# A fused attention, MLP and routed-expert kernel on Trainium2: the first expert's fifth slice split 256+128, and eight products of a slice planned behind the rows' high part alone

## The chip, the core and the metric

The program runs on one NeuronCore of a Trainium2 chip. Its engines are TensorE (PE in the profile; PEld is its weight load), VectorE (DVE), ScalarE (ACT), GpSimd (POOL) and SyncE (SP, which here issues most DMAs). The metric is the time of one execution in microseconds, the median of several runs; lower is better.

## The reference, cut to what matters

Chunked attention feeds a dense MLP, and that feeds eight experts with a fixed capacity of 384 tokens each (3072 tokens, 512 features, 1024 hidden features per expert):

```python
x = attention(q, k, v, mem_k, mem_v)            # 3072 x 512
x = leaky_relu(x @ w_in) @ w_out                # hidden 2048
order = argsort(-(x @ w_gate).flatten())        # greedy: best (token, expert) first
for e in range(8):                              # an expert closes at 384 tokens
    out[mask[e]] = relu(x[mask[e]] @ w1[e]) @ w2[e]
```

## The kernel before

Every product in fp32 is made of three: each operand is split into a high and a low part (`winh`, `winl`, `x1h`, `x1l`, `gh`, `gl`), and high by high, low by high and high by low are added up in PSUM. The high part is an ACT copy, the low part a VectorE subtraction.

The program has two phases. The first (up to some 670 us) is attention and the dense MLP. The second, `phase2`, treats the eight experts one after the other and at the same time finds out which tokens each of them gets. For the next expert, `search(p)` narrows a threshold in six levels. A level is a round trip: VectorE compares (`d` L284 or L291, `cm` L301), TensorE counts (L318), VectorE decides (`lc` L325, `jk` and `am` L333, `fl` L336), TensorE spreads the result over the partitions (L340), and the next level's `d` reads that. After the last level come `which`, `above`, `full` and `fill` (L362 to L415), after which `prep` (L258 to L273, ending in `oh`) begins the next search as one uninterrupted piece of VectorE work. `tail(p)` turns the set `F` into ranks (L429), slots (L437 to L444), indices (L467 on TensorE, L475 to L479 on VectorE), gathers the rows (GpSimd), transposes them (L487) and splits them (L490 on ACT, L494 on VectorE).

An expert's hidden features come in eight slices `f` of 128. For a slice `load` fetches 512 KB of weights and splits them (L610 on ACT, L612 on VectorE), `gemm1` makes twelve products into a PSUM tile `ph` (L630) and evacuates it as `gh` (L637 on ACT) and `gl` (L639 on VectorE), and `gemm2` adds `gh` and `gl` times the second weights into the accumulators `po` (L655). There are two `ph` tiles; a `ph` comes free when the `gl` that read it is done. The expert's 384 tokens are three tiles of 128. For the first expert the third tile arrives later than the other two, so its first `FA` slices are computed in two passes, on 256 tokens and later on 128 (`egbh` and `egbl` are the evacuations of the short pass); the other slices run on 384.

The order on each engine is not written by hand. Every step is put down as an operation with an estimated duration, its dependencies and a key; `Plan.run` is a list scheduler that always starts, on the engine that is free first, the ready operation with the lowest key. Search and tail have keys around -1000, `load` about 200 + 8p + f - 6, `gemm1` 200 + 8p + f, `gemm2` two more. So weight splits of the second expert's first slices (202, 203) come before the evacuation of the first expert's fifth slice (204) when both are ready. The planner's estimates set the order alone; at run time each engine takes its instructions in that order and waits on semaphores.

Of the kernel before, what the change touches and what calls it, by code (L numbers as in the profile page):

```python
# [214 lines left out]
def phase2(tc, P, C, ident, L, x2d, we, out, ps_h, ps_o, ps_y, pools, lready, xready, open_pools, open_experts, room, roomy, X0, rows, r_xt, r_g):  # L215
# [9 lines left out]
    KD = DM // 128  # L225
# [5 lines left out]
    HOLD = 2.0  # L231
    LATE, SLACK = 0.5, 0.7
    SW = 0.08
    FA = 4
    V, G, S = nc.vector, nc.gpsimd, nc.scalar
    R = [dict() for _ in range(E)]
    A = {}
# [272 lines left out]
    X, XT = {}, {}  # L510
# [107 lines left out]
    def gemm1(p, f, lo=0, hi=TB):  # L618
        s = NF * p + f
        P.key = 200 + s  # L620
        w, o = W[p, f]
        xs = X[p]
        c, k = slice(lo, hi), hi - lo
        ph = ps_h.take()
        gh, gl = (r.take() for r in (r_gb if lo else r_g))

        def mm(n):
            a, x = ((0, 0), (1, 0), (0, 1))[n // KD]
            d = n % KD
            nc.tensor.matmul(ph.t[:, :k], w[a].t[:, d * 128:(d + 1) * 128], xs[x].t[:, d, c],  # L630
                             start=(n == 0), stop=(n == 3 * KD - 1))

        t = []
        for n in range(3 * KD):
            t = [P.op(("T", {128: 0.112, 256: 0.122, TB: 0.178}[k]), lambda n=n: mm(n),
                      [o[0], XT[p][lo // 128:hi // 128], t], [ph, *w, *xs])]
        a = P.op(("S", 0.42), lambda: S.activation(gh.t[:, :k], ph.t[:, :k], AF.Relu),  # L637
                 [t, [] if p else open_experts], [ph, gh])
        b = P.op(("V", 0.47), lambda: V.scalar_tensor_tensor(  # L639
            gl.t[:, :k], ph.t[:, :k], 0.0, gh.t[:, :k].bitcast(FT), op0=OP.max, op1=OP.subtract), [a], [ph, gh, gl])  # L640
        for i in range(lo // 128, hi // 128):
            GL[s, i] = gh, gl, 128 * i - lo, [a, b]
# [3 lines left out]
    def gemm2(p, f, tiles=range(TT)):  # L646
        s = NF * p + f
        P.key = 200 + s + 2
        w, o = W[p, f]
        if f == 0 and p not in ACC:  # L650
            ACC[p] = [r.take() for r in ps_o]

        def mm(i, n, gh, gl, at):
            l, a = ((gh, 0), (gh, 1), (gl, 0))[n]
            nc.tensor.matmul(ACC[p][i].t, l.t[:, at:at + 128], w[a].t[:, 512:1024],  # L655
                             start=(f == 0 and n == 0), stop=(f == NF - 1 and n == 2))

        for i in tiles:
            gh, gl, at, done = GL.pop((s, i))
            if p == E - 1 and f >= NF - 2:  # L660
                P.key = 200 + NF * p + NF + 1 + i + (f - NF) / 4
            for n in range(3):
                q = PREV[i] = P.op(("T", 0.235), lambda i=i, n=n, gh=gh, gl=gl, at=at: mm(i, n, gh, gl, at), [done[:1 + n // 2], o[1], PREV.get(i)],
                                   [ACC[p][i], gh, gl, *w])
            if f < NF - 1:
                continue
            y = ps_y.take()
            o2 = P.op(("S", 0.53), lambda i=i, y=y: S.activation(y.t, ACC[p][i].t, AF.Copy), [q], [ACC[p][i], y])

            def fn(i=i, y=y):  # L670
                if stores:
                    G.memset(rt([1, 1], FT, "spacer"), 0.0)
                st = G.indirect_dma_start(
                    out=out, out_offset=bass.IndirectOffsetOnAxis(ap=R[p]["idx"][:, i:i + 1], axis=0),
                    in_=y.t, in_offset=None)
                for other in stores:
                    tc.declare_no_dep(st.ins, other.ins, reason="a token has one expert: rows of other tokens")
                stores.append(st)

            o2 = P.op(("G", 1.04), fn, [o2], [y])  # L680
            P.dep(P.op(("D", 1.05), None, (), [y]), [o2], lat=1.6)


    for p in range(E):
        if p < E - 1:
            search(p)
        else:
            P.key = -1000 + 10 * p
            filled[p] = P.op(("V", 1.0), lambda: last(p), chain, after=[gathered.get(p - 2)])
        number(p)  # L690
        tail(p)
        first = []
        if p == 0:
            for lo, hi in ((0, TB - 128), (TB - 128, TB)):
                tiles = range(lo // 128, hi // 128)
                for f in range(FA + 2):
                    if f < FA:
                        if lo == 0:
                            load(p, f)
                        gemm1(p, f, lo, hi)  # L700
                    if f >= 2:
                        gemm2(p, f - 2, tiles)
            first = range(FA)
        for f in range(NF):
            if f not in first:
                load(p, f)
                gemm1(p, f)
            s = NF * p + f - 2
            if s >= 0 and s not in first:
                gemm2(*divmod(s, NF))  # L710
        if p == E - 1:
            gemm2(p, NF - 2)
            gemm2(p, NF - 1)
# [3 lines left out]
def kernel(ctx, tc, q, k, v, w, w_gate_t, we, out):  # L717
# [515 lines left out]
    def expert_pools():  # L1233
# [7 lines left out]
    rows.view = lambda x: x.rearrange("p a b -> p (a b)").bitcast(FT)  # L1241
    o2 = P.op(("X", 0.0), expert_pools, [[d if t < NTILE - 1 else d.queue for t, d in X2D], list(PREV.values())])
    phase2(tc, P, C, ident, L, x2d, we, out, r_h, r_o, r_x2, pools, ls, X2D, o1, o2,
           [x.rearrange("p a b -> p (a b)") for x in win],
           [[GT[s] for s in range(SL * NF, NJ * NF)] + [[], list(PREV.values())][f >= 3] for f in range(NF // 2)], [r.take() for r in r_x1], rows, r_x1, r_g)
# [57 lines left out]
```

## Time and profile before

| | us |
|---|---|
| median of 3 runs | 988.23 |
| lowest and highest run | 986.81 to 990.12 |
| the profiled execution, whole | 989.57 |
| its span from first to last instruction | 987.6 |
| TensorE busy in the span | 969.7 |
| VectorE busy | 771.1 |
| ScalarE busy | 444.0 |

The profiled execution took 1.97 us more than its span, and 1.34 us more than the median. The profile's page gives busy times, the span in 40 slices, the chain of work that ended last and the costliest groups; the trace gives the instructions of any stretch in order of time, what each waited for, and busy times with the granted TensorE clock for any stretch.

### The profile page before, as it was taken

The numbers are of one execution on the slowest core, as the hardware profiler recorded it, in microseconds if no ns is written. First come the engines' busy times: TensorE is split into PE (matmuls) and PEld (weight loads), VectorE is DVE, ScalarE is ACT, GpSimd is POOL, SyncE is SP. The second block draws the span as 40 slices with busy tenths as digits, with TensorE's granted clock in tenths as the row PEclk, the third lists the DMA queues.
The fourth block names the chain that finished last, engine by engine and source line by source line (L and its number), as shares of the span: only waits on it lengthen the run. The fifth ranks groups of instructions, "written<-read, shape, count | busy, mean of one in ns | idle before, by whom it ended". The sixth has DMA issues, their size and how long they took to land.

```text
span 987.6 us, 17321 instructions
## 1 busy us (share of the span) xinstructions
PE 969.7 (98%) x6070; PEld 839.8 (85%) x6070; DVE 771.1 (78%) x2577; ACT 444.0 (45%) x1191; POOL 128.3 (13%) x145
## 2 busy tenths in 40 slices
PE   9999999999999999999999999998999999999997
PEld 7778888888888888888888999777888888888996
DVE  7999798698698689689779984587899998877610
ACT  7777634444444544444554433023424433435511
POOL 0678521000000000000000000010120120220211
PEclk9999999999999999999999999998999999999999
DMA  8656520011111121121120000045452642635500
GB/s 270 219 203 234 187 60 30 30 64 58 30 62 42 47 63 30 56 66 31 49 73 12 1 1 1 33 139 171 129 174 74 223 161 75 235 113 174 184 33 33
DMA packets 36327, 95.50 MB, mean 97 GB/s; under 512 B 4368, under 2 KB 8464, under 8 KB 36112
## 3 DMA queue, kind: packets, MB, share of 16 engines
q1 hardware_dynamic: 32256, 81.54, 25.3%
q0 software_dynamic: 3840, 12.59, 3.8%
q8 instruction: 48, 0.79, 0.3%
q14 instruction: 39, 0.32, 0.1%
q10 hardware_dynamic: 144, 0.26, 0.1%
HBM read 81.79 MB, written 12.58 MB: 96 GB/s over the span
## 4 chain that ended last, share of the span: by engine, by line
PE 83%; DVE 8%; issue 4%; ACT 2%; POOL 1%; DMA 1%; POOLq 0%; DVEq 0%; ACTq 0%; SPq 0%
PE po L1064 24%; PE ph L970 23%; PE ph L630 13%; PE po L655 12%; PE pa L852 3%; DVE junk L1094 2%; PE pa L922 2%; PE pa L895 2%; DVE wp L947 1%; DVE wa L949 1%; DMA wst<-in_w_dram 1%; PE pt L487 1%; DVE wp L946 1%; ACT X L861 1%; PE pc L318 1%
## 5 line engine op out<-in xcount | busy, mean ns | idle before, releaser
L1094 DVE CUSTOM_DVE_ANT_0 junk<-x,wgb 128x512 bf16<-128x512 f32 x296 | 207.6, 701 | 5.4 <-DMA wgb<-in_w_gate_t_dram 1.0
L978 ACT ACTIVATE gs<-ph 128x384 f32<-128x384 f32 x128 | 62.7, 490 | 185.2 <-PE ph L970 181.5
L1064 PE MATMUL po<-wouth,gh 128*128 128x512 f32 x321 | 130.8, 408 | 1.1 <-ACT wouth L953 0.9
L1064 PE MATMUL po<-woutl,gh 128*128 128x512 f32 x321 | 127.7, 398 | 1.7 <-POOL woutl L954 1.7
L979 DVE TENSOR_TENSOR gs<-ph,gs 128x384 f32<-128x384 f32 x128 | 71.1, 556 | 72.4 <-ACT gs L978 71.6
L1064 PE MATMUL po<-wouth,gl 128*128 128x512 f32 x321 | 126.5, 395 | 0.7 <-POOL gl L981 0.6
L861 ACT ACTIVATE X<-X,st 96x128 f32<-96x128 f32 x248 | 96.7, 392 | 47.8 <-DVE st L856 47.6
L970 PE MATMUL ph<-x1h,winh 128*128 128x384 f32 x512 | 111.3, 339 | 0.0
L970 PE MATMUL ph<-x1h,winl 128*128 128x384 f32 x512 | 110.7, 337 | 0.2 <-POOL winl L954 0.2
L970 PE MATMUL ph<-x1l,winh 128*128 128x384 f32 x512 | 109.6, 335 | 0.0
L970 PEld LDWEIGHTS ph<-x1h,winh 128*128 128x128 f32 x512 | 91.7, 188 | 9.2
L637 ACT ACTIVATE gh<-ph 128x384 fp32r<-128x384 f32 (+1 forms) x64 | 31.0, 485 | 142.7 <-PE ph L630 131.1
L970 PEld LDWEIGHTS ph<-x1h,winl 128*128 128x128 f32 x512 | 92.0, 188 | 1.9 <-POOL winl L954 0.8
L970 PEld LDWEIGHTS ph<-x1l,winh 128*128 128x128 f32 x512 | 90.6, 188 | 0.5
L1064 PEld LDWEIGHTS po<-wouth,gh 128*128 128x128 f32 x321 | 60.3, 188 | 14.9 <-ACT wouth L953 1.6
L1064 PEld LDWEIGHTS po<-wouth,gl 128*128 128x128 f32 x321 | 60.2, 188 | 14.9 <-POOL gl L981 2.0
L1064 PEld LDWEIGHTS po<-woutl,gh 128*128 128x128 f32 x321 | 60.3, 188 | 12.9 <-POOL woutl L954 3.0
L639 DVE SCALAR_TENSOR_TENSOR gl<-ph,gh 128x384 fp32r<-128x384 f32 (+1 forms) x64 | 34.9, 546 | 45.8 <-ACT gh L637 44.7
L980 ACT ACTIVATE gh<-gs 128x384 fp32r<-128x384 f32 x107 | 56.1, 524 | 31.9 <-DVE gs L979 31.6
L856 DVE CUSTOM_DVE_ANT_0 X<-pa,masks 96x128 f32<-96x128 f32 x232 | 56.0, 281 | 4.3 <-PE pa L852 4.3
L1180 POOL IOTA ij<- 128x128 int32 x1 | 0.2, 236 | 411.9 <-DVE L L1094 411.9
L981 DVE TENSOR_TENSOR gl<-gs,gh 128x384 fp32r<-128x384 f32 x83 | 45.8, 552 | 9.4 <-ACT gh L980 9.3
(260 smaller groups left out, 1948.0 us busy)
## 6 DMA issues: line engine op xcount, KB each, us to landing
west<-in_we_dram SPq DMA_DIRECT2D x56, 512.0 KB, 4.5
wst<-in_w_dram SPq DMA_DIRECT2D x32, 512.0 KB, 4.8
vt<-in_v_dram SPq DMA_DIRECT2D x30, 256.0 KB, 2.6
kt<-in_k_dram SPq DMA_DIRECT2D x30, 256.0 KB, 3.4
qt<-in_q_dram SPq DMA_DIRECT2D x31, 192.0 KB, 3.2
x2d<-x SPq DMA_DIRECT2D x21, 256.0 KB, 2.2
x<-in_we_dram SPq DMA_DIRECT2D x16, 256.0 KB, 2.8
wgb<-in_w_gate_t_dram SPq DMA_DIRECT2D x1, 2048.0 KB, 7.2
```

Source lines behind the costliest of these rows:

```text
L630: nc.tensor.matmul(ph.t[:, :k], w[a].t[:, d * 128:(d + 1) * 128], xs[x].t[:, d, c], start=(n == 0), stop=(n == 3 * KD - 1))
L639: b = P.op(("V", 0.47), lambda: V.scalar_tensor_tensor(gl.t[:, :k], ph.t[:, :k], 0.0, gh.t[:, :k].bitcast(FT), op0=OP.max, op1=OP.subtract ...
L655: nc.tensor.matmul(ACC[p][i].t, l.t[:, at:at + 128], w[a].t[:, 512:1024], start=(f == 0 and n == 0), stop=(f == NF - 1 and n == 2))
L856: V.tensor_tensor_reduce(out=X.t[:, h, :], in0=ps[h % 2].t[:QB, h // 2 * 128:h // 2 * 128 + 128], in1=masks[:, var, :], scale=-scale, scal ...
L861: S.activation(X.t[:, h, :], X.t[:, h, :], AF.Exp, bias=st.t[:, 0, h:h + 1], scale=-1.0, accum_out=st.t[:, 2, h:h + 1])
L970: nc.tensor.matmul(ph.t[:, :TB], win[wt][:, f, kk * 128:(kk + 1) * 128], xt.t[:, kk, :], start=(n == 0 and kk == 0), stop=(n == 2 and kk = ...
L978: o = P.op(("S", 0.37), lambda: S.activation(t.t, ph.t[:, :TB], AF.Copy, scale=0.01), [o], [ph, t], key=k)
L979: o = P.op(("V", 0.47), lambda: V.tensor_tensor(t.t, ph.t[:, :TB], t.t, op=OP.max), [o], [ph, t], key=k)
L980: x = P.op(("S", 0.42), lambda: S.activation(gh(), t.t, AF.Copy), [o, gd], [t, *gb], key=k)
L981: y = P.op({"V": 0.47} if j > 1 else {"V": 0.47, "G": 0.96} if j else {"G": 0.96}, lambda e=V if j > 1 else G: e.tensor_tensor(gl(), t.t, ...
L1064: nc.tensor.matmul(acc.t, lt()[:, sl], wout[wt][:, f, :], start=(f == 0 and n == 0), stop=(n == 2 and (f == NF - 1 or s == S6 - 1)), skip_ ...
L1094: V.tensor_tensor_reduce(out=pools["wgb"].tile([128, DM], BF, name="junk"), in0=x, in1=WGB[0][:, e, :], scale=1.0, scalar=0.0, op0=OP.mult ...
```

## The change

Two places in `phase2`. `FA`, the number of slices of the first expert that are computed in two passes (256 tokens, then 128), goes from 4 to 5. And in `gemm1` the planned dependency of a product on the rows: before, each of the twelve products waited in the plan for both parts (`x1h` and `x1l`) of the tiles that it reads; now the first eight (which read `x1h` only) wait for the high part alone, and the last four for both. The semaphores of the built program follow the tiles that are really read, so this second edit acts through the order that the planner finds; it holds for all experts.

```diff
-    FA = 4
+    FA = 5
...
-                      [o[0], XT[p][lo // 128:hi // 128], t], [ph, *w, *xs])]
+                      [o[0], [x[:1 + n // (2 * KD)] for x in XT[p][lo // 128:hi // 128]], t], [ph, *w, *xs])]
```

From the first expert's first product on, the order of TensorE, VectorE and ACT differs from before almost throughout. Two places matter here. The first is on TensorE, right after the first expert's third tile is transposed (L487). Before, the ranks (L429) and the short pass of slice 0 (128 wide) follow:

```order
L655 MATMUL po1_7582<-winl_119,gh_7620 128x512
L487 MATMUL pt_7708<-ident_95,xg2_7580 128x128 x4
L429 LDWEIGHTS ones_6571
L429 MATMUL pt_7732<-F_7670,ones_6571 128x24
L429 LDWEIGHTS tri_6569
L429 MATMUL pt_7732<-F_7670,tri_6569 128x24
L630 MATMUL ph_7745<-x1h_7396,winh_118 128x128
```

Now the 256-wide pass of the fifth slice (`ph_7728`) comes first, with the first count of the next search in the middle of it:

```order
L487 MATMUL pt_7709<-ident_95,xg2_7583 128x128 x4
L630 MATMUL ph_7728<-x1h_7396,winh_118 128x256 x4
L630 MATMUL ph_7728<-x1h_7396,winl_119 128x256 x4
L630 MATMUL ph_7728<-x1l_7406,winh_118 128x256
L318 LDWEIGHTS cm32_7724
L318 MATMUL pc_7744<-oh_7680,cm32_7724 128x32
...
L630 MATMUL ph_7728<-x1l_7406,winh_118 128x256 x3
L630 MATMUL ph_7765<-x1h_7396,winh_118 128x128 x2
L429 LDWEIGHTS ones_6571
```

Twelve products have moved ahead of the ranks; the tile `ph_7728` is the one that `gl_7717` reads before. On VectorE at the same moment, before, the end of `prep` is followed by the split of the third tile:

```order
L273 TENSOR_TENSOR oh_7680<-rev_6559,be_7679 128x192
L494 TENSOR_TENSOR x1l_7406<-pt_7708,x1h_7396 128x4x128
L284 SCALAR_TENSOR_TENSOR d_7721<-km_7685,zero_6573 128x48
L301 TENSOR_TENSOR cm32_7723<-thr0_6540,d_7721 128x768
L639 SCALAR_TENSOR_TENSOR gl_7730<-ph_7588,gh_7620 128x256
```

Now the evacuation that frees the fifth slice's `ph` follows `oh` directly, and the split comes after the first comparison:

```order
L273 TENSOR_TENSOR oh_7680<-rev_6559,be_7679 128x192
L639 SCALAR_TENSOR_TENSOR gl_7717<-ph_7589,gh_7621 128x256
L284 SCALAR_TENSOR_TENSOR d_7722<-km_7685,zero_6573 128x48
L301 TENSOR_TENSOR cm32_7724<-thr0_6540,d_7722 128x768
L494 TENSOR_TENSOR x1l_7406<-pt_7709,x1h_7396 128x4x128
L639 SCALAR_TENSOR_TENSOR gl_7742<-ph_7624,gh_7652 128x256
```

`gl` has moved from the fifth place to the second, but it still stands behind `oh`. The second place is on TensorE, some 7 us later, in the second and third level of the same search. Before, between the spreading of a level (L340) and the next count (L318) stand products of the expert, and behind the count the short passes of slices 1 and 2:

```order
L340 MATMUL pb_7698<-fl32_7768,ones_6571 128x1
L655 MATMUL po2_7789<-winh_118,egbh_7779 128x512
L655 MATMUL po2_7789<-winl_119,egbh_7779 128x512
L655 MATMUL po1_7582<-winh_118,gh_7652 128x512
L655 MATMUL po1_7582<-winl_119,gh_7652 128x512
...
L655 MATMUL po2_7789<-winh_118,egbl_7798 128x512
L318 LDWEIGHTS cm32_7793
...
L630 MATMUL ph_7828<-x1h_7396,winh_118 128x128 x4
L630 MATMUL ph_7828<-x1h_7396,winl_119 128x128 x4
L630 MATMUL ph_7828<-x1l_7406,winh_118 128x128 x4
```

Now, at the third level, the spreading, the count and the next spreading follow each other with nothing between (the six counts of 32 columns are cut to one here):

```order
L655 MATMUL po0_7573<-winl_119,gh_7768 128x512
L655 MATMUL po1_7580<-winh_118,gh_7768 128x512
L655 MATMUL po1_7580<-winl_119,gh_7768 128x512
L340 LDWEIGHTS ones_6571
L340 MATMUL pb_7698<-fl32_7835,ones_6571 128x1
L318 LDWEIGHTS cm32_7868
L318 MATMUL pc_7878<-oh_7680,cm32_7868 128x32
...
L340 LDWEIGHTS ones_6571
L340 MATMUL pb_7698<-fl32_7898,ones_6571 128x1
L630 MATMUL ph_7915<-x1h_7396,winh_118 128x128 x4
```

The short passes of slices 1 and 2 have moved behind that level. On VectorE there, now, the indices and the second expert's first weight splits (`wl0`, `wl1`) stand within the round trip:

```order
L336 TENSOR_SCALAR fl32_7835<-am32_7833 32x1
L612 TENSOR_TENSOR wl0_7850<-west_7715,wh0_7837 128x512
L475 TENSOR_SCALAR ix_7855<-pt_7841 32x12
...
L479 TENSOR_TENSOR idx_7854<-pt_7841,ix_7855 32x3 x4
L284 SCALAR_TENSOR_TENSOR d_7866<-km_7685,pb_7698,zero_6573 128x48
L301 TENSOR_TENSOR cm32_7868<-thr2_6544,d_7866 128x768
L612 TENSOR_TENSOR wl0_7850<-west_7715,wh0_7837 128x512
L612 TENSOR_TENSOR wl1_7874<-west_7719,wh1_7864 128x512
L325 TENSOR_TENSOR lc032_7889<-pc_7878,cap_6563 32x8
...
L336 TENSOR_SCALAR fl32_7898<-am32_7896 32x1
L612 TENSOR_TENSOR wl1_7874<-west_7719,wh1_7864 128x512
```

Before, at its third level, one split of `wl0` and one short evacuation stand there, and the short passes keep TensorE supplied meanwhile:

```order
L336 TENSOR_SCALAR fl32_7849<-am32_7847 32x1
L612 TENSOR_TENSOR wl0_7864<-west_7715,wh0_7826 128x512
L639 SCALAR_TENSOR_TENSOR egbl_7876<-ph_7828,egbh_7858 128x128
L284 SCALAR_TENSOR_TENSOR d_7882<-km_7685,pb_7698,zero_6573 128x48
L301 TENSOR_TENSOR cm32_7884<-thr2_6544,d_7882 128x768
```

Between `fl` and the third comparison, the indices and no short evacuation stand where one short evacuation stood.

## Rows read from the trace of the kernel before

**Rows 1.** The page, the span in 40 slices: granted TensorE clock in tenths.

```profile
PEclk9999999999999999999999999998999999999999
```

**Rows 2.** Waits of TensorE from 665 to 740 us: total, times, longest.

```profile
PE pt L429 <- DVE x1l L494: 2.1, 1, 2.1
PE ph L630 <- DVE fx L437: 0.9, 1, 0.9
```

**Rows 3.** Stretches: length, busy time of each engine, granted clock, DMA share, GB/s.

```profile
685.97:692.81 6.84, 6.84 (x33) 4.96 (x32) 4.11 (x21) 1.31 (x3) 0.00 (x0) 0.51 0.48 179
...
740.00:880.00 140.00, 140.00 (x877) 116.33 (x876) 126.55 (x454) 56.64 (x108) 18.96 (x27) 1.00 0.42 137
880.00:940.00 60.00, 60.00 (x324) 53.98 (x323) 36.72 (x80) 30.05 (x57) 13.42 (x18) 1.00 0.58 193
```

**Rows 4.** TensorE in order of time: start, duration, instruction, [idle before it <- releaser].

```profile
681.32 0.60 PE L487 MATMUL pt<-ident,xg 128*128 128x128 f32 x4
684.02 0.17 PE L429 MATMUL pt<-F,ones 128*128 128x24 bf16 x1 [2.10 <-DVE x1l L494]
...
685.16 0.30 PE L630 MATMUL ph<-x1h,winh 128*128 128x128 f32 x1 [0.94 <-DVE fx L437]
685.30 0.32 PE L318 MATMUL pc<-oh,cm 128*128 128x32 bf16 x6
685.46 0.53 PE L630 MATMUL ph<-x1h,winh 128*128 128x128 f32 x3
```

**Rows 5.** TensorE in order of time: products 256 and 128 wide, at full clock.

```profile
671.67 0.64 PE L630 MATMUL ph<-x1h,winl 128*128 128x256 f32 x4
672.15 0.64 PE L630 MATMUL ph<-x1l,winh 128*128 128x256 f32 x4
...
693.53 0.61 PE L630 MATMUL ph<-x1l,winh 128*128 128x128 f32 x4
693.97 0.61 PE L630 MATMUL ph<-x1h,winh 128*128 128x128 f32 x4
```

**Rows 6.** The chain that ended last: start, time on the chain, products 384 and 512 wide.

```profile
912.77 2.10 PE ph L630 x12
914.87 2.08 PE po L655 x9
```

**Rows 7.** VectorE in order of time, at the gap.

```profile
683.01 0.36 DVE L273 TENSOR_TENSOR oh<-rev,be 128x192 bf16<-128x192 f32 x1
683.29 0.68 DVE L494 TENSOR_TENSOR x1l<-pt,x1h 128x512 fp32r<-128x512 f32 x1
683.89 0.20 DVE L284 SCALAR_TENSOR_TENSOR d<-km,zero 128x48 bf16<-128x48 int32 x1
684.12 0.56 DVE L301 TENSOR_TENSOR cm<-thr,d 128x768 bf16<-128x768 bf16 x1
684.60 0.42 DVE L639 SCALAR_TENSOR_TENSOR gl<-ph,gh 128x256 fp32r<-128x256 f32 x1
```

**Rows 8.** VectorE in order of time, pieces of the next search's levels.

```profile
689.50 0.27 DVE L284 SCALAR_TENSOR_TENSOR d<-km,pb,zero 128x48 bf16<-128x48 int32 x1 [1.52 <-PE pb L340]
689.80 0.56 DVE L301 TENSOR_TENSOR cm<-thr,d 128x768 bf16<-128x768 bf16 x1
...
691.77 0.16 DVE L475 TENSOR_SCALAR ix<-pt 32x12 f32<-32x12 f32 x1 [0.87 <-PE pt L467]
...
693.08 0.15 DVE L325 TENSOR_TENSOR lc<-pc,cap 32x8 f32<-32x8 f32 x1
...
693.95 0.69 DVE L612 TENSOR_TENSOR wl<-west,wh 128x512 fp32r<-128x512 f32 x1
...
696.61 1.28 DVE L612 TENSOR_TENSOR wl<-west,wh 128x512 fp32r<-128x512 f32 x2
697.81 0.15 DVE L325 TENSOR_TENSOR lc<-pc,cap 32x8 f32<-32x8 f32 x1
```

**Rows 9.** ScalarE in order of time: weight splits of slices 4 to 6.

```profile
682.45 1.83 ACT L610 ACTIVATE winh<-x 128x512 fp32r<-128x512 f32 x3
```

## The prediction

> **What bounds the kernel now.** I read first the slices with the granted clock, then the waits of TensorE, then the stretch that they point to in order of time. The clock is full in all slices but one, near 680 us [rows 1]. TensorE is busy without a break in the long stretch of the experts [rows 3], so there the time is the sum of TensorE's work. The exception is one gap at the first expert: 2.10 us before L429 and 0.94 us before the first 128-wide product, with next to nothing between [rows 2, 4]. TensorE stops at 684.02 - 2.10 = 681.92 us and is in steady work again from 685.16. It waits for VectorE, which is at that time in one long uninterrupted piece that ends in `oh` [rows 7]. The gap has a second price: right after it the clock is granted at 0.51 for 6.84 us, which is its lower level of 1.2 GHz, against 2.4 GHz before and after [rows 3]. Half of 6.84 is 3.4 us. So this place costs the profiled execution about 3.04 + 3.4 = 6.4 us. Any change to the order here has to be weighed against these 6.4 us; elsewhere TensorE's work alone counts.
>
> **Part 1: the gap is only partly filled.** The fifth slice's 256-wide pass now stands directly behind the transposes. Its weights are there: ScalarE splits them without any idle time before it [rows 9], and in the new order it does so ahead of the third tile's rows. What is not there is the PSUM tile. There are two of them, and the one wanted is free after `gl_7717`, which VectorE has behind `oh`. VectorE leaves `oh` at 683.29 [rows 7]; a 256-wide `gl` takes 0.42 us, so it ends at 683.71. In the trace TensorE started 0.14 us after the end of such a `gl` (684.60 + 0.42 = 685.02, against 685.16) [rows 4, 7]. The fifth slice starts at 683.85. The idle time is 1.93 us instead of 3.04: **-1.1 us**. After that TensorE has nine products of 0.12 us each (0.48 for four) [rows 5], a count of 0.16 us [rows 4] and three products more, up to 685.45; VectorE meanwhile does `d` (0.23), `cm` (0.48), the split (0.60) and the second `gl` (0.42) one after the other, which ends by 685.44 [rows 7]. The 128-wide pass can follow without a gap worth counting.
>
> **Part 2: the clock at this gap.** Before, 3.04 us of idle time in a stretch of 3.24 brought the clock down. An unbroken 1.93 us, followed by steady products, is a good third less, so I expect the clock to stay up here: **-3.4 us**, with 0 as the other end.
>
> **Part 3: a new pocket at the third level.** The products that filled the search's round trips before are used up or moved back, and TensorE has spreading, count and spreading in a row. Prices on VectorE, from start to start: `lc` to `fl` 0.87 (693.08 to 693.95), the indices 1.31 (691.77 to 693.08), `d` 0.30 (689.50 to 689.80), a weight split 0.60 (two from 696.61 to 697.81) [rows 8]; `cm` takes 0.56 and holds the engine for 0.48 [rows 7]. First half: from the end of the second count VectorE has to do `lc` to `fl`, one split, the indices, `d` and `cm`, that is 0.87 + 0.60 + 1.31 + 0.30 + 0.56 = 3.64, and some 0.3 us for two hand-overs of the 0.14 us above; TensorE has eight products of 0.231 [rows 6] and some 0.27 us of small ones (an estimate), 2.1 us. Idle 1.8 us at least; since a few VectorE steps of the slots stand ahead of `lc`, it may be up to 0.5 us more (an estimate). I take 2.1. Second half: after `cm` VectorE does two splits (1.20) and `lc` to `fl` (0.87 and the end of `fl`) before the next spreading, while TensorE has a count of 0.16 us: 0.48 + 1.20 + 0.87 + 0.17 less 0.56 + 0.14 + 0.16 makes 1.9 us. After it twelve products of 0.11 us [rows 5], 1.33 us, stand against a split, a `gl`, `d` and `cm`: 0.60 + 0.42 + 0.30 + 0.56 + 0.14 = 2.0, begun some 0.4 us earlier; 0.3 us more. Together **+4.3 us**, between 3.0 (the bare round trips) and 4.8. Neither engine can get round it: what could fill it stands behind the waiting instruction on TensorE.
>
> **Part 4: the clock at the pocket.** The pocket is 4.0 us idle with 0.16 us of counting in it; the gap before was 3.04 us with about as little. Whatever brought the clock down there is here in greater measure. I take the same price, **+3.4 us**, with ends of 0 and 5 (the products after it are 128 wide and less dense, so the low stretch may last longer).
>
> The Trainium skill, page "TensorE: Matmul & The Clock Gate", section "What's actually happening", says that the moment at which the clock changes is not tied to the kernel's start and falls differently from run to run. No single trace can show that; by it a pocket of this size may cost 0 in one execution and 3.4 in another, which is the first rival below. [...]
>
> **Part 5: the split slice and the rest.** Twelve products of 384 tokens, 2.10 us [rows 6], become twelve of 256 and twelve of 128: 1.44 + 1.33 = 2.77. **+0.7 us** on TensorE, which is the bound. The additional evacuation falls on ScalarE and VectorE; VectorE is busy 126.55 of 140 us later on [rows 3], and nothing waits for it there. The second edit changes no instruction, and in the trace no product waited for `x1l` where `x1h` was enough, except in the gap. Of the later search levels I set TensorE's work in each round trip against VectorE's in the new order and found no other bare one; I leave 0.5 us on either side.
>
> **Sum.** -1.1 - 3.4 + 4.3 + 3.4 + 0.7 = +3.9 us. Against the profiled execution that is 989.57 + 3.9 = 993.5; that execution lay 1.34 above the median, and so I place the forecast on the median: 988.23 + 3.9 = **992.1 us**.
>
> **The rivals.**
> (a) Not slower: the clock stays up at the pocket too. The idle time is in two pieces of some 2 us with a count between, neither longer than the 2.10 that began the gap before. Then Part 4 is 0 and the sum is +0.5: 988.7. It decides whether the low stretch is lost in both kernels or only in the one before. Against it: the two pieces together are longer than before's.
> (b) The change does not do at the first gap what it says: 1.93 us is still enough for the clock. Then TensorE is about 3.4 us late when it comes to the pocket; VectorE waits there for it, and the first half shrinks to `d`, `cm` and two hand-overs, 1.1 instead of 2.1. Sum 3.9 + 3.4 - 1.0 = +6.3: 994.5. For it: the piece before L429 alone was 2.10.
> (c) Faster: the clock stays up everywhere and the pocket is smaller by 3 us or more, since the splits wait for nothing and VectorE runs ahead. The rows give the bare round trips alone 3 us, so this would need a clear error in Part 3; below 985.
>
> **How the numbers follow.** A measurement of this kernel tells some 0.3%, 3.0 us, from no change. Forecast 0.55, (a) 0.24, (b) 0.16, (c) 0.05. The forecast's own spread is about 1.2 us (Part 3's ends, 0.5 for the rest), so one in six of its cases lies within 3.0 us. Slower: 0.46 + 0.16 + 0.02 of (a) = 0.64. Within: 0.09 + 0.21 = 0.30. Faster 0.06. The range reaches from (a) less 1.1 us to (b) plus 0.5: 987.6 to 995.0.
>
> **What would show it.** In the profile after: a wait of about 1.9 us of a 256-wide L630 for `gl` at 682 to 684 us; full clock from 684 to 691; then a wait of 2 us of L318 for `cm` and one of 1.9 us of L340 for `fl` near 691 to 695, and a stretch of some 7 us at the lower clock behind them. If there is a low stretch right after 684, it is (b); if there is none at all, (a). The forecast is wrong if TensorE has no wait for VectorE in the third level, or if new waits show up after 700 us.

## The result, and the profile after

| | us |
|---|---|
| kernel before, median beside it | 989.28 |
| changed kernel, median of 6 runs | 1003.22 |
| lowest and highest run | 1001.06 to 1004.75 |
| ratio to before | 1.0137, 95% interval 1.0123 to 1.0151 |
| the profiled execution, whole | 1004.75 |
| its span from first to last instruction | 1002.8 |
| TensorE busy in the span | 978.7 |

The change makes the kernel 13.9 us slower. Forecast were 992.1 us, +3.9, and at most 995.0: the sign is right, and the time lies far outside the range. The changed kernel was run twice more among the experiments, with medians of 1000.36 and 1002.33, that is 10.7 and 12.8 us above the kernel before beside it. The forecast misses by 7 to 10 us.

The page gives the first hint. The slices with the granted clock, to be held against [rows 1]:

```profile
PEclk9999999999999999999999999998799999999999
```

Two slices are low now, around 700 us, where one was low before, near 680. The waits of TensorE from 665 to 740 us (total, times, longest), against [rows 2]:

```profile
PE ph L630 <- DVE gl L639: 2.2, 1, 2.2
PE pb L340 <- DVE fl L336: 1.7, 1, 1.7
PE pc L318 <- DVE cm L301: 1.7, 1, 1.7
```

These are the three waits that the prediction names. TensorE in order of time at the third level and behind it:

```profile
694.32 0.17 PE L340 MATMUL pb<-fl,ones 32*128 32x1 bf16 x1
696.20 0.33 PE L318 MATMUL pc<-oh,cm 128*128 128x32 bf16 x6 [1.71 <-DVE cm L301]
698.24 0.16 PE L340 MATMUL pb<-fl,ones 32*128 32x1 bf16 x1 [1.71 <-DVE fl L336]
698.33 1.12 PE L630 MATMUL ph<-x1h,winh 128*128 128x128 f32 x4
699.24 1.05 PE L630 MATMUL ph<-x1h,winl 128*128 128x128 f32 x4
...
715.37 1.16 PE L630 MATMUL ph<-x1h,winh 128*128 128x384 f32 x3
```

The four 128-wide products that took 0.61 us in [rows 5] take 1.05 here. VectorE meanwhile has no gap; it does in the two waits what the order put there:

```profile
693.23 0.69 DVE L612 TENSOR_TENSOR wl<-west,wh 128x512 fp32r<-128x512 f32 x1
693.96 0.16 DVE L475 TENSOR_SCALAR ix<-pt 32x12 f32<-32x12 f32 x1
...
695.28 0.28 DVE L284 SCALAR_TENSOR_TENSOR d<-km,pb,zero 128x48 bf16<-128x48 int32 x1
695.59 0.56 DVE L301 TENSOR_TENSOR cm<-thr,d 128x768 bf16<-128x768 bf16 x1
696.06 1.28 DVE L612 TENSOR_TENSOR wl<-west,wh 128x512 fp32r<-128x512 f32 x2
```

The stretches (length, busy time of each engine, granted clock, DMA share, GB/s), against [rows 3]:

```profile
686.00:694.32 8.32, 7.54 (x61) 6.15 (x61) 7.67 (x33) 5.16 (x11) 0.00 (x0) 1.00 0.70 253
696.34:716.82 20.48, 18.77 (x95) 16.60 (x93) 12.91 (x39) 4.30 (x10) 2.66 (x3) 0.50 0.38 129
```

Behind the first gap the clock stays full, as forecast. It falls at 696.34, behind the pocket's first wait and ahead of its second, and stays low for 20.48 us, three times as long as the 6.84 us in [rows 3]. TensorE was busy in 18.77 of them; the other 1.71 are the second wait. Finally, the waits of TensorE from 740 to 940 us, where the kernel before has none:

```profile
PE pb L340 <- DVE fl L336: 1.5, 2, 1.1
PE pc L318 <- DVE cm L301: 1.0, 1, 1.0
PE pb L340 <- DVE am L333: 0.8, 1, 0.8
```

That is 3.3 us which no part of the prediction has. So two questions are open: why the clock stays low for so long, and where the late waits come from.

### The profile page after: what moved, and what is told of

It is laid out like the page before. It is cut to its first block, busy times and chain, and to the rows that moved or that the text cites. A ratio compares the mean times of both kernels' runs of the same rounds, so it can differ in the third digit from the quotient of the medians.

```text
span 1002.8 us, 17339 instructions
## 1 busy us (share of the span) xinstructions
PE 978.7 (98%) x6082; PEld 847.5 (85%) x6082; DVE 771.9 (77%) x2578; ACT 444.1 (44%) x1192; POOL 129.9 (13%) x145
## 4 chain that ended last, share of the span: by engine, by line
PE 78%; DVE 8%; issue 7%; ACT 3%; DMA 2%; POOL 1%; another core or an unknown queue 0%; POOLq 0%; DVEq 0%; ACTq 0%
PE po L1064 24%; PE ph L970 23%; PE ph L630 11%; PE po L655 9%; PE pa L852 3%; DMA wst<-in_w_dram 2%; PE pa L922 2%; PE pa L895 2%; DVE junk L1094 2%; ACT X L861 1%; DVE wp L947 1%; DVE wa L949 1%; PE pt L487 1%; PE pc L318 1%; POOL out_dram L673 1%
## 5 line engine op out<-in xcount | busy, mean ns | idle before, releaser
L1064 PEld LDWEIGHTS po<-wouth,gl 128*128 128x128 f32 x321 | 60.3, 188 | 15.2 <-POOL gl L981 2.2
```

The costliest lines, as they stand in the source:

```text
L1064: nc.tensor.matmul(acc.t, lt()[:, sl], wout[wt][:, f, :], start=(f == 0 and n == 0), stop=(n == 2 and (f == NF - 1 or s == S6 - 1)), skip_ ...
```

## The experiments

**Which of the two edits makes the pocket.** Each was built alone. The first edit alone:

```diff
-    FA = 4
+    FA = 5
```

> Only the first edit: FA is 5, the planned dependency of the products stays as it was. In the built order the third level's count and spreading have products of the expert between them again, and behind the third tile's transposes the ranks (L429) stand first, as in the kernel before. Theory (the second edit makes the pocket, the first alone does not): the first gap is about as before, 3 us idle with some 7 us at the lower clock behind it, no wait of more than 0.5 us at the third level, +0.7 us for the split slice: 989 to 991 us, full clock from 695 on. Rival (five split slices drain the products whatever the planned dependency): a pocket of 3 us and about 20 us at the lower clock, near 1003 us.

Measured: 989.78 us, ratio 1.0004 (0.9991 to 1.0017): no change. The stretches of its trace:

```profile
680.00:690.00 10.00, 7.05 (x53) 5.64 (x52) 9.47 (x43) 3.71 (x8) 0.00 (x0) 1.00 0.81 280
690.00:717.00 27.00, 27.00 (x198) 23.08 (x197) 24.20 (x86) 11.77 (x26) 3.09 (x3) 1.00 0.39 118
```

The first gap is there (2.95 us not busy in 10), the pocket is not, as the theory has it. It is wrong on one point: nearly the same gap as in [rows 4] brought no low clock in this execution. The second edit alone:

```diff
-                      [o[0], XT[p][lo // 128:hi // 128], t], [ph, *w, *xs])]
+                      [o[0], [x[:1 + n // (2 * KD)] for x in XT[p][lo // 128:hi // 128]], t], [ph, *w, *xs])]
```

> Only the second edit: FA is 4. In the built order a short pass stands behind the transposes, the first gap is one wait of about 1.9 us for gl, and a pocket with a bare round trip (spreading, count) stands not in the first expert's short passes but some 55 us later, at a level of the third search. Theory (the price of a pocket is the clock, and the clock comes back fast where 384 and 512 wide products follow): the pocket costs 2 to 2.5 us idle and no more than some 7 us at the lower clock (3.4 us); the first gap gives back 1.1 + 3.4 us: 985 to 989 us. Rival (a pocket costs some 20 us at the lower clock whatever follows it): about 995 us.

Measured: 995.38 us, ratio 1.0060 (1.0042 to 1.0078). Its pocket, TensorE in order of time, and the two low stretches of its trace:

```profile
729.77 0.32 PE L318 MATMUL pc<-oh,cm 128*128 128x32 bf16 x6 [2.66 <-DVE cm L301]
730.83 1.65 PE L630 MATMUL ph<-x1h,wh 128*128 128x384 f32 x4 [0.75 <-DVE gl L639]
```

```profile
686.02:692.84 6.82, 6.82 (x31) 5.79 (x26) 3.95 (x19) 1.59 (x4) 0.00 (x0) 0.50 0.60 229
...
730.39:733.80 3.41, 2.97 (x9) 2.97 (x10) 2.84 (x10) 0.00 (x0) 2.71 (x4) 0.50 0.72 207
```

The time is the rival's, about 995 us, but not for the rival's reason. The rival has some 20 us at the lower clock, whatever follows; here a single wait of 2.66 us, longer than each of the two in the changed kernel, and 0.75 us more brought 3.41 us of it, and 384-wide products followed. That much of the theory holds. Its time failed on two points: the pocket was 3.4 us idle instead of 2 to 2.5, and the expectation took the first gap's clock as won, where it was low for 6.82 us as before. The second edit is what opens pockets, in both orders.

**Is the low clock the pocket's?** The two waits were filled with products that nobody reads (their target lies beside the count, in the same PSUM tile):

```diff
+    def spare(t, n): [nc.tensor.matmul(t[:, 128:], X0[0].t[:, 0, :128], X0[0].t[:, 0], start=True, stop=True) for _ in range(n)]
...
-        r["pc"] = pools["ps_r"].tile([128, K * E], FT, name="pc")
+        r["pw"] = pools["ps_r"].tile([128, 512], FT, name="pc"); r["pc"] = r["pw"][:, :K * E]; spare(r["pw"], 9 * ((p, n) == (2, 2)))
...
-        part = int(n >= UPPER)
+        part = int(n >= UPPER); spare(R[p]["pw"], 9 * ((p, n) == (2, 2)))
```

> The changed kernel with 9 additional products of 384 columns (results not used, written beside the count in its PSUM tile) in front of the third level's count and 9 more in front of the spreading behind it, 1.57 us each time, in the two waits of 1.71 us. Nothing else in the order changes. Theory (the low clock of about 20 us is the pocket's, by the idle time): the clock stays full through 697 to 717 us, the twenty 128-wide passes take 0.11 us a product, and the time falls by about 10 us to 993 us, with some 0.3 us of waiting added back. Rival 1 (the low clock belongs to the short passes and transposes themselves, idle time or not): the clock falls all the same within 697 to 717 and the time stays at 1002 to 1004 us. Rival 2 (the additional products delay the count): the same clock gain, but over 1 us of new waits, 995 us.

Measured: 993.95 us, 9.3 less than the changed kernel. TensorE in order of time, and the stretch behind:

```profile
695.57 1.86 PE L246 MATMUL pc<-x1h 128*128 128x384 f32 x9
697.29 0.32 PE L318 MATMUL pc<-oh,cm 128*128 128x32 bf16 x6
699.16 1.84 PE L246 MATMUL pc<-x1h 128*128 128x384 f32 x9 [1.54 <-DVE am L333]
```

```profile
699.00:717.00 18.00, 17.84 (x141) 15.92 (x142) 15.81 (x47) 6.92 (x15) 1.40 (x2) 1.00 0.49 161
```

The second nine products wait until VectorE has read the count, so that wait stays (1.54 us), and they lie on the path behind it: rival 2 is right there, at about the 1.6 us that they take. All the same the clock is full throughout this stretch, and the 128-wide passes behind run at full speed. It is not luck of one execution: over the whole span the granted clock is 0.993 or more in all ten executions of this kernel, and 0.990 or less in all fourteen of the changed one. So these passes do not bring the clock down; the pocket does. It does not need both its waits for that: in the changed kernel's own trace the clock fell between the two. One wait of 1.54 us did not bring it down here, and why one such wait does and another does not stays open.

**Why it stays low.** Both waits were left as they are, and 24 products of 384 columns put right behind them (the tile as above):

```diff
-                         start=(n in (0, UPPER)), stop=(n in (UPPER - 1, NL - 1)), skip_group_check=True)
+                         start=(n in (0, UPPER)), stop=(n in (UPPER - 1, NL - 1)), skip_group_check=True); spare(R[p]["pw"], 24 * ((p, n) == (2, 2)))
```

> The changed kernel with 24 additional products of 384 columns (results not used) right behind the second wait of the pocket, ahead of the 128-wide passes; the two waits stay. They take 4.2 us at full clock, 8.4 us at half. Theory (what follows the pocket decides how long the clock stays low: 128-wide passes keep it low, wide products bring it back): the clock is back by some 705 us, with the short passes behind it at full speed; the time is 1003.2 + 7 - 9 = about 1001 us, between 999 and 1003. Rival (the pocket itself decides): the clock stays low for some 20 us as before, and the products cost up to 8.4 us: 1010 to 1012 us.

And for comparison 38 products of 128 columns in the same place, 4.2 us of work as well (against the lines of the wide ones; of the last line only the end is shown):

```diff
-    def spare(t, n): [nc.tensor.matmul(t[:, 128:], X0[0].t[:, 0, :128], X0[0].t[:, 0], start=True, stop=True) for _ in range(n)]
+    def spare(t, n): [nc.tensor.matmul(t[:, 128:256], X0[0].t[:, 0, :128], X0[0].t[:, 0, :128], start=True, stop=True) for _ in range(n)]
...
-skip_group_check=True); spare(R[p]["pw"], 24 * ((p, n) == (2, 2)))
+skip_group_check=True); spare(R[p]["pw"], 38 * ((p, n) == (2, 2)))
```

> The counterpart of the kernel with 24 wide products behind the pocket: the same place, but 38 additional products of 128 columns (results not used), which take 4.2 us at full clock and 8.4 us at half, like the 24 wide ones. Theory (it is the width of what follows that brings the clock back, not additional work or time): the clock stays low through the additional products and the short passes behind them, some 25 us in all, and comes back only where the 384 and 512 wide products follow each other; the time is that of the changed kernel plus 7 to 8 us, 1007 to 1010 us. Rival (any uninterrupted work of this length behind the pocket brings the clock back): full clock within some 4 to 7 us behind the pocket and a time near that of the wide ones, 996 to 999 us.

Measured: 996.67 us with the wide ones, 1008.97 with the narrow ones. The stretches with the wide products:

```profile
697.83:701.25 3.42, 3.42 (x13) 3.42 (x12) 1.74 (x3) 0.00 (x0) 0.14 (x1) 0.50 1.00 381
701.25:717.00 15.75, 15.75 (x132) 14.10 (x131) 11.33 (x34) 6.45 (x15) 0.00 (x0) 1.00 0.17 45
```

and with the narrow ones:

```profile
692.94:720.24 27.30, 25.59 (x128) 23.52 (x128) 11.62 (x37) 4.30 (x10) 2.69 (x3) 0.50 0.28 97
720.24:780.00 59.76, 59.76 (x374) 49.94 (x372) 55.31 (x205) 22.77 (x43) 7.30 (x10) 1.00 0.41 133
```

With the wide products the low stretch is 3.42 us long, and the kernel is 3.7 us faster than the changed one beside it (1000.36), although it does 4.2 us of useless work. With the narrow ones it is 27.30 us long, and the clock rises where it does in the changed kernel, once 384-wide products have begun behind a run of 512-wide ones. Theory and time agree for the narrow ones. With the wide ones the time is some 4 us below the expected 1001, which was worked out from 1003.2 with its 3.3 us of late waits; this trace has none. So it is shown: the pocket brings the clock down, and the row of short passes behind it is gone through at half speed. The forecast's price of 6.84 us was read behind a gap that twelve 128-wide and then nine 512-wide products followed.

**The late waits.** The changed kernel was run again, to see whether they return:

> The changed kernel once more, for a second profiled execution. Theory (the low stretch behind the pocket and the late waits are both part of the changed kernel): two waits of 1.7 us at the third level, some 20 us at the lower clock from about 697 us on, and again some 3 us of new waits of TensorE after 777 us; 1003 us. Rival (the late waits belong to that one execution: the kernel with the pocket filled has the same order on every engine and none of them): the low stretch again, but less than 1 us of waits after 777 us.

> The changed kernel a third time, beside the one with narrow products on the same chip. Theory: the two waits of 1.7 us at the third level, 17 to 20 us at the lower clock behind them, no new waits of TensorE after 740 us, 1000 to 1003 us. Rival (the late waits belong to the changed kernel and the second execution was the exception): again about 3 us of waits at 780, 826 and 866 us.

Measured: 1000.36 and 1002.33 us. The low stretch is there in both traces (second, then third execution):

```profile
685.35:688.76 3.41, 3.16 (x19) 3.07 (x20) 2.35 (x9) 0.63 (x1) 0.00 (x0) 0.50 0.86 321
699.00:716.07 17.07, 17.07 (x83) 15.00 (x83) 10.10 (x29) 4.29 (x10) 0.69 (x1) 0.50 0.37 127
```

```profile
684.00:693.00 9.00, 7.68 (x61) 6.22 (x61) 8.21 (x38) 5.79 (x11) 0.27 (x1) 1.00 0.60 222
696.66:713.73 17.07, 17.07 (x82) 14.90 (x82) 10.45 (x28) 4.32 (x11) 0.16 (x1) 0.50 0.33 116
```

The late waits are not there in both: the second execution has none of them, the third has 2.7 us. In the third, VectorE and then TensorE:

```profile
777.08 0.68 DVE L612 TENSOR_TENSOR wl<-west,wh 128x512 fp32r<-128x512 f32 x1
780.32 0.27 DVE L284 SCALAR_TENSOR_TENSOR d<-km,pb,zero 128x48 bf16<-128x48 int32 x1 [2.56 <-PE ph L630]
```

```profile
777.58 0.17 PE L340 MATMUL pb<-fl,ones 32*128 32x1 bf16 x1
...
781.24 0.32 PE L318 MATMUL pc<-oh,cm 128*128 128x32 bf16 x6 [1.73 <-DVE cm L301]
```

`d` reads what the spreading at 777.58 wrote, and nothing stands ahead of it on VectorE from 777.76 on; it starts 2.56 us later all the same. It does not need the products in between: in the second execution, at the same place, it starts 0.04 us after the spreading has ended, with 1.7 us of them still to run. ScalarE is late too: `gh` starts 0.91 us behind the end of the products that it reads, 0.04 us in the second execution. So TensorE's results reach the other engines late, and no work explains it. These places lie where GpSimd issues the gathers of one expert and the stores of another back to back (0.30 us apart near 774 us, and 3.72 us in the kernel before), which the changed order brought together. So the stores of the first seven experts were left out:

```diff
-                if stores:
-                    G.memset(rt([1, 1], FT, "spacer"), 0.0)
+                if p < E - 1: return G.memset(rt([1, 1], FT, "spacer"), 0.0)
+                if stores: G.memset(rt([1, 1], FT, "spacer"), 0.0)
```

> The changed kernel without the stores of the first seven experts' rows (L673; the indirect stores that GpSimd issues are left out, so these rows of the output are not written; TensorE, VectorE, ScalarE and SyncE keep their order). In the changed order these stores stand right beside the gathers of the next expert on GpSimd (in the kernel before they were done some 4 us ahead of the gathers), and VectorE's late steps of the search fell into these stretches. Theory (where GpSimd issues stores and gathers back to back, TensorE's results reach VectorE up to 2 us late, in some executions): no wait of TensorE over 0.5 us after 740 us; two waits of 1.7 us and 17 to 20 us at the lower clock as before; 999 to 1001 us. Rival (the late waits come and go by themselves or hang on the gathers): waits of 1 us or more near 780, 826 or 866 us, as in two of the three executions of the changed kernel.

> The same kernel, without the first seven experts' stores, once more for a second profiled execution. Theory: again no wait of TensorE over 0.5 us after 740 us. Rival: waits of 1 us or more near 780, 826 or 866 us in at least one of the two.

Measured: 999.14 us and, once, 999.17; no wait of TensorE after 740 us in either trace, and 17.06 and 20.48 us at the lower clock. That fits the theory, but does not prove it: of six executions with the changed order and the stores, three had no late wait either (the second run, the one with filled waits and the one with wide products; the one with narrow products had 3.1 us). Nor has the trace of the second edit alone one, though in its order too gathers and stores follow each other within 0.3 us at four experts. What delays the hand-over stays open.

**Taking the first gap away.** In the kernel before, the gap was first filled with products that nobody reads (`spare` as above, a tile of the search that is free then):

```diff
-        r["ps"] = pools["ps_t"].tile([128, 2, NTILE], FT, name="pt")
+        t = pools["ps_r"].tile([128, 512], FT, name="pc") if p == 1 else None; spare(t, 10 * (p == 1)); r["ps"] = pools["ps_t"].tile([128, 2, NTILE], FT, name="pt")
...
-            nc.tensor.matmul(r["ps"][:, n], C[0][x], r["F"], start=True, stop=True)
+            nc.tensor.matmul(r["ps"][:, n], C[0][x], r["F"], start=True, stop=True); spare(t, 4 * n * (p == 1))
```

> The kernel before with 14 additional products of 384 columns (results not used, in a PSUM tile of the search that is free then): 10 in front of the ranks, 1.75 us in the wait of 2.10 us, and 4 behind them, 0.70 us in the wait of 0.94 us. Theory (the 6.84 us at the lower clock come from this gap): full clock from 684 to 693, time 988.2 - 3.4 = 984.8 us. Rival 1 (the products end late and push the ranks back): up to 1 us less gain, 985.8 us. Rival 2 (transposes and narrow products bring the clock down there anyway): no change, 988 us.

Measured: 987.10 us, ratio 0.9979 (0.9968 to 0.9989). The stretch of its trace:

```profile
680.00:690.00 10.00, 9.31 (x72) 7.62 (x70) 9.17 (x45) 3.58 (x7) 0.00 (x0) 1.00 0.76 261
```

The clock is full and 0.69 us are left idle. The gain is 2.5 us instead of 3.4. The low clock behind the gap need not come in every execution of the kernel before: the first edit alone had nearly the same gap and no low clock, and the granted clock of the 25 executions of the kernel before that were run beside it lies between 0.991 and 0.997 (0.994 in the profiled execution of [rows 3]). So the full 3.4 us was probably too high a price for it on average; that is argued, not shown.

Then the cause was taken away: `gl` no longer waits for `prep` and the search, in the kernel before and in the changed one, by one more key in `gemm1`:

```diff
-            gl.t[:, :k], ph.t[:, :k], 0.0, gh.t[:, :k].bitcast(FT), op0=OP.max, op1=OP.subtract), [a], [ph, gh, gl])
+            gl.t[:, :k], ph.t[:, :k], 0.0, gh.t[:, :k].bitcast(FT), op0=OP.max, op1=OP.subtract), [a], [ph, gh, gl], key=None if p else -2000)
```

> The kernel before with one change: the gl evacuations of the first expert's slices get a key that puts them ahead of the search on VectorE. In the built order one of them moves ahead of the end of the search and of prep, so that six products of 512 columns (1.4 us) of the first expert stand behind the third tile's transposes, and the 256-wide products that used to wait for prep no longer do. Theory (the gap of 3 us is only gl behind prep, and the clock falls there only because of the gap): 1 us or less idle near 682 to 686 us, full clock: 989.6 - 2.5 - 2 = about 985 us. Rival 1 (the search is now later and its round trips open somewhere else): waits of 2 us or more at the next levels, 988 to 991 us.

> The changed kernel with the same one-line change of the key. Theory (the loss of the change is the pocket that its order opens, not the split slice or the planned dependency as such): where the gl evacuations come first, the built order has products between the spreading and the count of every level, no pocket, no low clock near 700 us, and the time is that of the kernel before with this key plus 0.7 us for the split slice: 985 to 987 us. Rival (five split slices and the late rows cost by themselves): 992 us or more.

Measured: 983.39 us on the kernel before, ratio 0.9930 (0.9911 to 0.9949), and 984.56 us on the changed one, ratio 0.9947 (0.9931 to 0.9963). Neither trace has a wait of TensorE between 665 and 940 us. The stretches of the first, then of the second:

```profile
680.00:690.00 10.00, 9.95 (x74) 8.70 (x72) 9.36 (x42) 2.33 (x6) 0.00 (x0) 1.00 0.69 242
690.00:720.00 30.00, 30.00 (x203) 25.85 (x203) 27.89 (x85) 16.12 (x32) 4.63 (x5) 1.00 0.42 131
```

```profile
680.00:690.00 10.00, 10.00 (x78) 9.11 (x76) 9.46 (x39) 2.81 (x7) 0.00 (x0) 1.00 0.71 234
690.00:720.00 30.00, 30.00 (x207) 25.73 (x207) 27.32 (x83) 16.10 (x32) 4.32 (x6) 1.00 0.38 125
```

On the kernel before, the place of the gap now reads (TensorE in order of time):

```profile
683.45 0.60 PE L487 MATMUL pt<-ident,xg 128*128 128x128 f32 x4
683.81 0.48 PE L655 MATMUL po<-winh,gh 128*128 128x512 f32 x1
...
685.29 0.56 PE L630 MATMUL ph<-x1h,winh 128*128 128x128 f32 x4
```

Six 512-wide products stand where TensorE waited. With the key, both edits together cost 1.2 us: the 13.9 us are the price of the order that the edits led to, of its pocket and, in some executions, its late waits, and not of the split slice or of the planned dependency as such. The kernel before with the key is the fastest version here, 6.3 us ahead of the kernel before.

## Why the prediction was wrong, point by point

Spans and busy times of the page tell where the time went. Against [rows 3] and the page of before (span 987.6, TensorE busy 969.7), the three executions of the changed kernel have a span longer by 15.2, 10.8 and 12.4 us, of which TensorE is busy for 9.0, 8.3 and 7.8. The prediction had 3.9, of which 0.7 busy (0.7 for the slice, and the clock's 3.4 won and lost again).

| step | forecast | measured, three executions |
|---|---|---|
| Part 1, idle at the first gap | -1.1 | 2.17, 2.27 and 2.18 for 3.04: -0.9, -0.8, -0.9 |
| Part 2, clock there | -3.4 | full, 3.41 us low, full: -3.4, -1.7, -3.4 |
| Part 3, the pocket, idle | +4.3 | 3.42, 3.37 and 3.46 |
| Part 4, clock at the pocket | +3.4 | half of 18.77, 17.07 and 17.07 busy: +9.4, +8.5, +8.5 |
| Part 5, split slice | +0.7 | 1.2 between the two kernels with the key, with some 2 us of spread |
| Part 5, the rest | 0 | late waits 3.3, none, 2.7 |

Added up by kind, the terms make +8.4, +9.2 and +7.5 us of busy time (the slice taken at 0.7, and 1.7 each time for one more low stretch of 3.4 us: near 614 us in the first two, at 782 us behind a late wait in the third) against the 9.0, 8.3 and 7.8 measured, and 5.8, 2.6 and 5.3 us of idle time against 6.2, 2.5 and 4.6. So most of what is missing from the forecast is clock: 8.3, 7.6 and 7.1 us more of busy time than its 0.7, where the whole span is 11.3, 6.9 and 8.5 us longer than forecast. The rest, in the first and third, is idle time, that of the late waits.

**Bound, Parts 1 and 3: right.** The bound was read rightly, and the three waits are the ones foretold, in place and releaser. The halves of the pocket are 1.71 us each for 2.1 and 1.9: no step of the slots stood ahead of the decision, and the first bound, 1.8, was the better one. The 0.3 us behind did not come: with TensorE's products there at half speed VectorE had time enough.

**Part 2: right in two of three, but not a fixed price.** With one and the same order and a wait of 2.2 us the clock stayed full or was low for 3.41 us; behind the kernel before's gap it was low for 6.84 us, and behind the like gap of the first edit alone not at all. The Trainium skill, page "TensorE: Matmul & The Clock Gate", section "What's actually happening", has the moment of the change fall differently from run to run; these traces agree with it. A clock term read from one execution is an outcome, not a price.

**Part 4: the step that failed.** It took the price of one low stretch for that of another: 6.84 us, so +3.4 us, with an upper end of 5. Measured are 17 to 20.5 us at the lower clock in five executions with this order, with the stores or without them, and so 8.5 to 9.4 us of time. The parenthesis at its end names the reason, but gives it 1.6 us of room; 128-wide passes, with some 512-wide products and transposes among them, ran at half speed for 17 us behind the pocket, and the runs with wide and with narrow products show that what follows sets the length. Rival (a), that the clock stays up, was given 0.24 and did not happen in any of these five. Rival (b) named the right kind of loss, but at the first gap.

**Part 5, the rest: wrong in size, by 3 us in two of three executions.** The search of the later levels for a bare round trip found none, and there is none: the second execution and those with filled waits or wide products run through without a wait there. In the other two of the three, results of TensorE came late. The prediction's sentence that it would be wrong if new waits showed up after 700 us has come true, and for a reason that the order does not show.

One term is in no part: in five of the fourteen executions with a trace the clock was low for 3.4 us near 614 us, in the phase that the change does not touch, with TensorE busy throughout. The profiled execution of the kernel before had none.

## What to carry to other kernels

Price a new idle spot by what TensorE runs behind it, not by what the last idle spot cost: here the same pocket cost 3.4 us at the lower clock with wide products behind it, 17 to 20 us with narrow ones, and nothing, in one trace, with the first of its two waits filled. Before slices are split to fill a gap, ask why the releasing instruction is late: one key that let the evacuation pass the search brought 6.3 us, and the fill 2.5. Where a static order decides, a bare round trip (spreading, count, spreading with nothing between) can be read off it before it is run.

## What the runs showed of the hardware

That TensorE at 0.50 of its clock stays there while it is busy without a break was not expected: 17.07 us of 17.07 in two executions, and 25.59 of 27.30 with more narrow products. The same 128-wide passes at full clock did not bring it down (17.84 us busy in 18.00 at 1.00). Nor does it take a wait to lose the clock, as the first edit's trace shows in the phase before the experts. TensorE had no wait from 605 us on, but ran 18 products of 8 columns in the 3 us before the clock fell (TensorE in order of time, then the stretch):

```profile
609.50 0.83 PE L1024 MATMUL pl<-sel,x 16*128 16x8 f32 x6
610.26 0.83 PE L1029 MATMUL pl<-wog,gs 128*128 128x8 f32 x6
...
611.75 0.73 PE L1029 MATMUL pl<-wog,gs 128*128 128x8 f32 x6
```

```profile
612.50:615.92 3.42, 3.42 (x11) 3.23 (x11) 0.20 (x1) 0.49 (x1) 0.00 (x0) 0.50 0.00 0
```

And a result of TensorE can reach VectorE 2.56 us late, with VectorE free for it; it was seen in three executions with the changed order, at places where GpSimd's stores and gathers stand back to back, and its cause is open.
